# Sums of four rows of V, q and k as TensorE products with bands of ones

## The chip, the cores and the metric

The kernel runs on one core of a Trainium2 chip. The metric is the device time of one execution in microseconds (us), the median of repeated runs; lower is better.

## The reference

Three blocks follow each other. The first, attention, runs for 4 batches of 8 heads over 576 positions of 64 features; the second and third are dense products whose weights are far larger.

```python
q_d = q.reshape(B, H, Sd, 4, D).mean(axis=3)     # Sd = 144; the same for k and v
out_d = sm_attn(q_d, k_d, v_d)                   # softmax(q_d k_d' / 8) v_d
out_up = np.repeat(out_d, 4, axis=2)
mask = np.abs(pos[:, None] - pos[None, :]) < 4   # a local attention beside it
out_local = softmax(where(mask, q k' / 8, -1e9)) v
x = out_up + out_local                           # heads side by side: 4 x 576 x 512
h = np.maximum(x @ w_in, 0)                      # 512 -> 1024
h = h * sigmoid(conv3(h)) @ w_out                # 1024 -> 512
u = x + (x' @ U @ V)'                            # x is now that h; rank 32 over the positions
out = u + np.maximum(u @ w_ch1, 0) @ w_ch2       # 512 -> 2048 -> 512
```

The change is in the first lines: the sums of four neighbouring rows of q, k and V that stand behind the means.

## The kernel before

The heads are worked on two at a time: 16 pairs, p = 0 to 15, four pairs to a batch. One pair has its two heads (h = 0, 1) in the two halves of the 128 partitions.

Of q and k, a load brings 96 rows to each of six column blocks (`load_qk`, tiles qr and kr, two buffers each). `transposes` turns the six blocks on PE into PSUM (tile tr), `emit_qc` and `emit_kc` copy them to SBUF for the local attention, and `emit_qsum` and `emit_ksum` add groups of four columns with a DVE reduction (tiles qs and ks). qs is then scaled into a block-diagonal tile qdbd by POOL, ACT or DVE. `emit_S` makes the local scores of a pair (tile S, 20 products in ten windows of 64 keys, after a product of the mask with identR), `emit_Sd` the scores of the pooled attention (tile Sd). Maxima on DVE, exponentials on ACT (`emit_E`, `emit_Ed`), normalisation on DVE or POOL (`emit_norm`), then transposes of the probabilities on PE (`emit_T`, tiles P and Pd into T).

V is loaded twice. `load_vw` brings ten windows of 64 rows for each head into vw, a tile with one buffer, in four transfers; the local product O = P V of `emit_PV` reads it (20 products a pair). `load_vr` brings the same rows again into vr, 72 partitions with 2 x 4 rows each; `emit_vd` adds them by fours on POOL, in three instructions, into vd, which `emit_PVd` reads (four products into the same bank). `emit_x` adds the two attentions on DVE, and `prep_x` splits the result into a high and a low part (tile xhl) for the product with w_in.

From there on PE does large products: `g1` with w_in (tile g or gb, 12 products to a part, 48 parts; its first may start when pairs 0 to 3 are through), `g2` with w_out (tile acc), then the third block (L935 to L1027). Weights come as 64-bit words and are decoded on ACT and DVE (`decode`, tiles w1t, wraw, wst) and split (`split_hi` on ACT, `split_lo` on DVE or POOL). All loads are issued on SP's queue, in program order, so a load that waits for its buffer holds those behind it.

The order of everything is a hand-kept list of words, `CFG["SEQ"]`: each word is one step of one pair or part (aqT.3 is the transposes of q of pair 3, alw.3 its load of vw, aPVa.3 and aPVb.3 its V products, aPd.3 its PVd, wd a step of decoding, 1.0 a quarter of the first part of g1), and each engine runs its instructions in that order. Words that begin with d are dummy products of the mask (`spin`) whose result is not used. The banks of PSUM for S, Sd, T and O are taken in turn from one ring of four (`bank`); the transposes of whole q and k have two tiles of their own until g1 begins.

## Time and profile before

| | |
|---|---|
| time, median of 3 runs | 781.85 us (780.24 to 782.37) |
| profiled execution | 780.98 us, its span 779.1 us |
| PE busy | 745.5 us, 96% of the span |
| DVE, ACT, POOL busy | 432.3, 339.7, 176.9 us |
| DMA | 51.03 MB, 66 GB/s in the mean |

Busy time is the time in which an engine has at least one instruction in work. A PE that is busy is not a PE at its peak: its matmuls are pipelined, so the distance between two starts is the better price of one. A product of 32-bit numbers is two PE instructions in the trace, so the 20 products of a pair are counted as x40; a transpose is one. The columns of the views by stretches are the busy time of each engine with its number of instructions, then the granted clock of PE, the busy share of the 16 DMA engines and their rate.

### The profile page before, as it was taken

How to read it: one execution, taken by the hardware profiler on the slowest of the kernel's cores; microseconds unless marked ns; L12 is line 12 of the kernel's file. 1: busy time of each engine (PE TensorE's matmuls, PEld its weight loads, DVE VectorE, ACT ScalarE, POOL GpSimd, SP SyncE). 2: the span in 40 equal slices, each digit the busy share in tenths (PEclk: the TensorE clock that was granted, in tenths of full speed). 3: DMA queues.
4: the chain of work that ended last, by engine and by line, in shares of the span. 5: the costliest groups of instructions: out<-in, count | busy, mean ns of one | idle time of the engine just before them, and what ended most of it. 6: DMA issues, size and time to landing. Idle time of an engine off the chain costs nothing.

```text
span 779.1 us, 13059 instructions
## 1 busy us (share of the span) xinstructions
PE 745.5 (96%) x5068; PEld 663.4 (85%) x5068; DVE 432.3 (55%) x827; ACT 339.7 (44%) x1023; POOL 176.9 (23%) x246
## 2 busy tenths in 40 slices
PE   5678999999999999999999999999999999999997
PEld 4556878889888888998898999999899999989996
DVE  6899898888887888899987312211221221122111
ACT  4678978787666766677444212111111211111110
POOL 2357656534336151113611000000000000000000
PEclk9999999999999999999999999999999999999999
DMA  9779664354232122111243100000010000001001
GB/s 227 158 169 205 154 132 96 80 93 92 60 115 53 52 82 82 54 44 39 87 156 121 57 1 1 19 22 1 1 40 1 1 16 25 1 1 41 1 0 42
DMA packets 82450, 51.03 MB, mean 66 GB/s; under 512 B 62013, under 2 KB 74581, under 8 KB 82389
## 3 DMA queue, kind: packets, MB, share of 16 engines
q1 hardware_dynamic: 82388, 50.21, 25.6%
q8 instruction: 40, 0.66, 0.3%
q14 instruction: 22, 0.17, 0.1%
HBM read 45.47 MB, written 4.72 MB: 64 GB/s over the span
## 4 chain that ended last, share of the span: by engine, by line
PE 79%; DVE 11%; ACT 7%; issue 1%; DMA 1%; SPq 0%; POOL 0%; DVEq 0%; ACTq 0%; POOLq 0%
PE acc L1027 25%; PE gb L1008 12%; PE g L1008 12%; PE acc L901 10%; PE g L839 8%; PE gb L839 3%; ACT P L491 2%; DVE hc L875 2%; PE O L594 2%; DVE w1t L217 1%; PE S L477 1%; PE tr L385 1%; PE Sd L513 1%; PE O L605 1%; PE ut L994 1%
## 5 line engine op out<-in xcount | busy, mean ns | idle before, releaser
L1027 PE MATMUL acc<-w,a 128*128 128x512 f32 x864 | 215.0, 393 | 0.0
L1027 PEld LDWEIGHTS acc<-w,a 128*128 128x128 f32 x864 | 161.0, 188 | 29.4 <-DVE a L1017 0.2
L901 PE MATMUL acc<-w,ghl 128*128 128x512 f32 x432 | 111.4, 396 | 0.1
L1008 PE MATMUL g<-uT,w 128*128 128x384 f32 x576 | 111.2, 339 | 0.0
L1008 PE MATMUL gb<-uT,w 128*128 128x384 f32 x576 | 110.9, 339 | 0.0
L1008 PEld LDWEIGHTS g<-uT,w 128*128 128x128 f32 x576 | 101.9, 188 | 4.0
L1008 PEld LDWEIGHTS gb<-uT,w 128*128 128x128 f32 x576 | 101.7, 188 | 3.2 <-POOL w L229 0.2
L1017 DVE SCALAR_TENSOR_TENSOR a<-gb,a 128x384 fp32r<-128x384 f32 x48 | 26.7, 557 | 131.5 <-ACT a L1016 131.5
L839 PE MATMUL g<-xhl,w 128*128 128x386 f32 (+1 forms) x456 | 93.6, 345 | 0.6 <-ACT hc L850 0.3
L901 PEld LDWEIGHTS acc<-w,ghl 128*128 128x128 f32 x432 | 79.5, 188 | 14.7 <-POOL ghl L892 0.5
L1017 DVE SCALAR_TENSOR_TENSOR a<-g,a 128x384 fp32r<-128x384 f32 x48 | 26.7, 557 | 116.5 <-ACT a L1016 116.5
L839 PEld LDWEIGHTS g<-xhl,w 128*128 128x128 f32 x456 | 79.6, 189 | 5.2 <-ACT hc L850 1.8
L1016 ACT ACTIVATE a<-gb 128x384 fp32r<-128x384 f32 x48 | 23.5, 490 | 136.0 <-PE gb L1008 119.6
L1016 ACT ACTIVATE a<-g 128x384 fp32r<-128x384 f32 x48 | 23.5, 490 | 133.3 <-PE g L1008 133.3
L875 DVE SCALAR_TENSOR_TENSOR hc<-hc,cw 128x384 f32<-128x384 f32 x96 | 65.4, 684 | 8.4 <-ACT hc L869 6.4
L491 ACT ACTIVATE P<-S,nm 122x64 f32<-122x64 f32 x160 | 47.7, 317 | 5.6 <-DVE nm L484 5.2
L892 POOL TENSOR_TENSOR ghl<-hc,ghl 128x384 fp32r<-128x384 f32 x21 | 25.3, 1207 | 92.8 <-ACT ghl L889 53.6
L879 ACT ACTIVATE hc<-hc 128x384 f32<-128x384 f32 x48 | 25.0, 524 | 21.4 <-DVE hc L875 20.9
L491 ACT ACTIVATION_READ_ACCUMULATOR P<-S,nm 122x1 f32 x160 | 33.6, 210 | 0.0
L889 ACT ACTIVATE ghl<-hc 128x384 fp32r<-128x384 f32 x48 | 25.2, 524 | 18.5 <-DVE hc L884 17.0
L884 DVE SCALAR_TENSOR_TENSOR hc<-hc 128x384 f32<-128x384 f32 x48 | 30.3, 635 | 4.8 <-ACT hc L879 4.4
L869 ACT ACTIVATE hc<-hc,cw 128x384 f32<-128x384 f32 x48 | 29.5, 615 | 0.9
(135 smaller groups left out, 1013.3 us busy)
## 6 DMA issues: line engine op xcount, KB each, us to landing
wraw<-in_moe_w_ch_dram SPq DMA_DIRECT2D x29, 512.0 KB
qr<-in_q_dram SPq DMA_DIRECT2D x32, 144.0 KB
kr<-in_k_dram SPq DMA_DIRECT2D x32, 144.0 KB
vr<-in_v_dram SPq DMA_DIRECT2D x16, 288.0 KB
out_dram<-u SPq DMA_DIRECT2D x17, 256.0 KB
w1t<-in_moe_w_in_dram SPq DMA_DIRECT2D x8, 512.0 KB
w1t<-in_moe_w_out_dram SPq DMA_DIRECT2D x8, 512.0 KB
vw<-in_v_dram SPq DMA_DIRECT2D x32, 128.0 KB
```

Of the source, the lines that this page charges most:

```text
L491: nc.scalar.activation(out=e["P"][:, i, h], in_=e["S", h][:122, i], func=AF.Exp, bias=e["nm"][:, h, i:i + 1], accum_out=e["sm"][:, i, h:h ...
L839: nc.tensor.matmul(p[:, :wd], w[:, a, cc], xhl[g, cc][:, b, :wd], start=k == 0, stop=k == 3 * NCC - 1)
L869: nc.scalar.activation(out=flat(g, c), in_=inner(g, hts[n], 0), func=AF.Copy, scale=cw[:, f:f + 1])
L875: nc.vector.scalar_tensor_tensor(out=o, in0=inner(g, hts[n], k), scalar=cw[:, k * NF + f:k * NF + f + 1], in1=o, op0=ALU.mult, op1=ALU.add)
L884: nc.vector.scalar_tensor_tensor(out=o, in0=o, scalar=1.0, in1=inner(g, hts.pop(n), 1), op0=ALU.add, op1=ALU.mult)
L889: nc.scalar.activation(out=t[:, 0], in_=cts[n], func=AF.Copy)
L892: eng.tensor_tensor(ghl[n][:, 1], cts.pop(n), ghl[n][:, 0].bitcast(F32), op=ALU.subtract)
L901: nc.tensor.matmul(acc[g][c], t[:, a, c * P:(c + 1) * P], w[:, b], start=f == 0 and i == 0, stop=f == NF - 1 and i == 2)
L1008: nc.tensor.matmul(p[:, :TB], w[:, a, cc], uT[g, cc][:, b, :TB], start=k == 0, stop=k == 3 * NCC - 1)
L1016: nc.scalar.activation(out=t[:, 0], in_=p[:, :TB], func=AF.Relu)
L1017: nc.vector.scalar_tensor_tensor(out=t[:, 1], in0=p[:, :TB], scalar=0.0, in1=t[:, 0].bitcast(F32), op0=ALU.max, op1=ALU.subtract)
L1027: nc.tensor.matmul(acc2[g][c], t[:, a, c * P:(c + 1) * P], w[:, b], start=f == 0 and i == 0, stop=f == NF2 - 1 and i == 2)
```

## The change

For pairs 0 to 7 the second load of V and the three additions on POOL are gone. Instead `emit_Vp` multiplies the windows in vw with bands of ones: for each of ten windows and two heads one product, the band (64 rows, 72 columns) as weights and the window's 64 features moving, added up in two PSUM banks, one per head (tile vp). `emit_Vc` copies the two banks to vd, on ACT, DVE or one on each. Four bands are built on POOL at the start (sixteen small memsets and selects, with those of `fours`). vd now lies with contiguous groups, so `emit_T` takes contiguous columns of Pd for these pairs.

For q and k of pairs 0 to 3 `pooled` makes the sums on PE: the six blocks as weights, as for their transposes, and a 96 x 24 matrix of ones in fours as the moving side. The scaling into qdbd then reads PSUM, on DVE or ACT, and ks is copied from PSUM on DVE or ACT. The word aksa now means this copy on ACT (it was the same as aks before).

The list of words is new as a whole. It has 2585 words instead of 2579; besides the new words, some evictions, normalisations, subtractions and weight splits change their engine, and there are five dummy products instead of seven.

```diff
-        "akT.0 aqv.0 akc.0 aS.0 aks.0 dq.1 aM0.0 wl.1 wd.1 wo.2 aM1.0 aE14.0 aE02.0 aSd.0 wd.1 aE04.0 aMd.0 wd.1 "
...
+    SEQ="wl.0 wd.0 dS.0 wd.0 wd.0 wd.0 lc C wl.2 wd.2 wd.2 wd.2 wh.0 wd.2 wh.2 wo.2 alq.0 aqT.0 aqp.0 aqc.0 aqs.0 "
+        "aVp.1 aVcv.1 aPVa.1 aE0.3 wd.7 akc.4 wd.7 aPd.1 aPVb.1 aT0.2 axd.1 axa.1 ax.1 wh.7 wo.7 av0.2 aS.4 aT1.2 "
...
@@ -274,6 +275,31 @@
         nc.gpsimd.memset(t[:, S:], 0.0)
         qTs.append(t)
 
+    NVP, NG = 8, 72
+    band = p0.tile([P, 4, 160], F32, name="band")
+    nc.gpsimd.memset(band, 0.0)
+    for i, (a, ng) in enumerate(((0, 14), (1, 15), (3, 14), (8, 14))):
+        t = band[:, i, NG:NG + 32].rearrange("p (h x) -> p h x", h=2)[:, :, :ng]
+        nc.gpsimd.memset(t, 1.0)
+        nc.gpsimd.affine_select(out=t, in_=t, pattern=[[-64, 2], [-4, ng]], base=-a, channel_multiplier=1,
+                                compare_op=ALU.is_ge, fill=0.0)
+        nc.gpsimd.affine_select(out=t, in_=t, pattern=[[64, 2], [4, ng]], base=3 + a, channel_multiplier=-1,
+                                compare_op=ALU.is_ge, fill=0.0)
+    NPQ = 4
+    fours = p0.tile([96, 24], F32, name="fours")
+    nc.gpsimd.memset(fours, 1.0)
+    nc.gpsimd.affine_select(out=fours, in_=fours, pattern=[[-4, 24]], base=0, channel_multiplier=1,
+                            compare_op=ALU.is_ge, fill=0.0)
+    nc.gpsimd.affine_select(out=fours, in_=fours, pattern=[[4, 24]], base=3, channel_multiplier=-1,
+                            compare_op=ALU.is_ge, fill=0.0)
+    GROUP = [0] + [(QB * i - i % 2 * 2) // 4 for i in range(1, 9)] + [130]
+    BAND = [0] + [2 - i % 2 for i in range(1, 9)] + [3]
     PT = pa.tile([P, 5, 122], F32, name="PT")
 
     X = {}
@@ -385,6 +411,14 @@
                 nc.tensor.transpose(view[c // 3][:, (c % 3) * 96:(c % 3 + 1) * 96],
                                     e[nm + "r"][:, c].rearrange("p h d -> p (h d)"), ident[:96, :96])
 
+    def pooled(p, nm):
+        e = st[p]
+        t = e[nm + "4"] = whole_tile(p, nm)[:, 0, 288:288 + SD]
+        for c in range(6):
+            nc.tensor.matmul(t[:, 24 * c:24 * c + 24], e[nm + "r"][:, c].rearrange("p h d -> p (h d)"), fours,
+                             start=True, stop=True)
     def like(ap, src):
 
         return ap if len(src.shape) == 2 else ap.rearrange("p (a x) -> p a x", a=2)
@@ -409,14 +443,18 @@
         if not 0 <= p < NPAIR:
             return
         e = st[p]
-        if "qs" not in e:
-            e["qs"] = p0.tile([P, SD], F32, name="qs", tag="qs")
-        qs = e["qs"]
-        for c, src in e["qps"]:
-            nc.vector.tensor_reduce(out=like(qs[:, c.start // 4:c.stop // 4], src), in_=quads(src),
-                                    op=ALU.add, axis=AX.X)
-        if c.stop < S:
-            return
+        if "q4" in e:
+            qs = e["q4"]
+            eng = "DVE" if eng == "Pool" else eng
+        else:
+            if "qs" not in e:
+                e["qs"] = p0.tile([P, SD], F32, name="qs", tag="qs")
+            qs = e["qs"]
+            for c, src in e["qps"]:
+                nc.vector.tensor_reduce(out=like(qs[:, c.start // 4:c.stop // 4], src), in_=quads(src),
+                                        op=ALU.add, axis=AX.X)
+            if c.stop < S:
+                return
         qd = qdbds[p % 2]
         for h in range(2):
             dst = qd[64 * h:64 * h + 64, :, 48 * h:48 * h + 48]
@@ -436,13 +474,16 @@
         for c, src in e["kps"]:
             copy(like(e["kT"][:, c], src), src)
 
-    def emit_ksum(p):
+    def emit_ksum(p, copy=nc.vector.tensor_copy):
         if not 0 <= p < NPAIR:
             return
         e = st[p]
         if "ks" not in e:
             e["ks"] = p0.tile([P, SD], F32, name="ks", tag="ks", bufs=2)
         ks = e["ks"]
+        if "k4" in e:
+            copy(ks, e["k4"])
+            return
         for c, src in e["kps"]:
             nc.vector.tensor_reduce(out=like(ks[:, c.start // 4:c.stop // 4], src), in_=quads(src),
                                     op=ALU.add, axis=AX.X)
@@ -457,6 +498,23 @@
             nc.gpsimd.tensor_tensor(vr[:, h, :, 0:2], vr[:, h, :, 0:2], vr[:, h, :, 2:4], op=ALU.add)
         nc.gpsimd.tensor_tensor(vd, vr[:, :, :, 0], vr[:, :, :, 1], op=ALU.add)
         e["vd"] = vd
+    def emit_Vp(p):
+        e = st[p]
+        e["vps"] = [bank([P, 512], "vp") for _ in range(2)]
+        for i in range(10):
+            c = i // 5
+            for h in range(2):
+                x = NG * (c + 1) + 16 * h - GROUP[i]
+                nc.tensor.matmul(e["vps"][h][:NG, c * D:c * D + D], band[64 * h:64 * h + 64, BAND[i], x:x + NG],
+                                 e["vw"][64 * h:64 * h + 64, i], start=i % 5 == 0, stop=i % 5 == 4)
+    def emit_Vc(p, copies):
+        e = st[p]
+        vd = e["vd"] = pa.tile([72, 2, 2, D], F32, name="vd", tag="vd", bufs=2)
+        for h, copy in enumerate(copies):
+            copy(vd[:, h].rearrange("p c d -> p (c d)"), e["vps"][h][:NG, :2 * D])
 
     def emit_S(p):
 
@@ -560,7 +618,8 @@
                                     e["P"][:, SB[m].start + j].rearrange("p h x -> p (h x)"), ident[:122, :122])
         for j, x in enumerate(((), (0, 1), (2, 3, 4, 5))[m]):
             c = 96 * j + (248 if m == 1 else 0)
-            nc.tensor.transpose(ps[:72, c:c + 96], e["Pd"][:, x // 2, x % 2::2], ident[:96, :96])
+            cols = slice(NG * (x % 2), NG * (x % 2) + NG) if p < NVP else slice(x % 2, None, 2)
+            nc.tensor.transpose(ps[:72, c:c + 96], e["Pd"][:, x // 2, cols], ident[:96, :96])
 
     def emit_Tc(p, m, copy=nc.scalar.copy, copy2=None):
         if not 0 <= p < NPAIR:
@@ -702,7 +761,8 @@
         "kT": (3, lambda p: transposes(p, "k")), "qT": (4, lambda p: transposes(p, "q")),
         "kT0": (3, lambda p: transposes(p, "k", 0)), "kT1": (3, lambda p: transposes(p, "k", 1)),
         "qT0": (4, lambda p: transposes(p, "q", 0)), "qT1": (4, lambda p: transposes(p, "q", 1)),
-        "kc": (3, lambda p: emit_kc(p, A)), "kv": (3, lambda p: emit_kc(p, V)), "ks": (3, emit_ksum), "ksa": (3, emit_ksum),
+        "kc": (3, lambda p: emit_kc(p, A)), "kv": (3, lambda p: emit_kc(p, V)), "ks": (3, emit_ksum), "ksa": (3, lambda p: emit_ksum(p, A)),
+        "kp": (3, lambda p: pooled(p, "k")), "qp": (4, lambda p: pooled(p, "q")),
         "qc": (4, emit_qc), "qv": (4, lambda p: emit_qc(p, True)), "qs": (4, emit_qsum), "qsv": (4, lambda p: emit_qsum(p, "DVE")), "qsa": (4, lambda p: emit_qsum(p, "ACT")),
         "lq": (5, lambda p: load_qk(p, "q")), "lk": (4, lambda p: load_qk(p, "k")),
         "lw": (1, load_vw), "lv": (2, load_vr), "vd": (1, emit_vd),
@@ -723,6 +783,8 @@
             for j in range(5):
                 OPS[f"E{m}{j}"] = 2, lambda p, m=m, j=j: emit_E(p, m, j)
     OPS["S"] = 2, emit_S
+    OPS["Vp"], OPS["Vc"] = (0, emit_Vp), (0, lambda p: emit_Vc(p, (A, A)))
+    OPS["Vcv"], OPS["Vcb"] = (0, lambda p: emit_Vc(p, (V, V))), (0, lambda p: emit_Vc(p, (A, V)))
 
 
     NK = conv_w.shape[0]
```

Two places of PE's order. First the start, from the transposes of pair 0 on (tr: transposes of qr and kr; S and Sd: scores). Before:

```order
L368 MATMUL tr<-mask,identR 128x320
L385 MATMUL tr<-ident,qr 128x96 x6
L385 MATMUL tr<-ident,kr 128x96 x6
L471 MATMUL S<-mask,identR 128x320 x2
L477 MATMUL S<-kT_128,qT_131 58x64 x20
L368 MATMUL tr<-mask,identR 128x320
L513 MATMUL Sd<-ks,qdbd_129 96x144 x3
L385 MATMUL tr<-ident,kr 128x96 x6
L385 MATMUL tr<-ident,qr 128x96 x6
```

The same place now (fours: the sums of q and k):

```order
L411 MATMUL tr<-ident,qr 128x96 x6
L419 MATMUL tr<-fours,qr 128x24 x6
L411 MATMUL tr<-ident,kr 128x96 x6
L419 MATMUL tr<-fours,kr 128x24 x6
L394 MATMUL S<-mask,identR 128x320
L529 MATMUL S<-mask,identR 128x320 x2
L535 MATMUL S<-kT_128,qT_131 58x64 x20
L394 MATMUL tr<-mask,identR 128x320
L571 MATMUL Sd<-ks,qdbd_129 96x144 x3
```

The sums of pairs 0 and 1 have come in behind each transpose, and fewer dummy products stand between. The second place is between the V products of pair 1 and of pair 2 (O<-PT,vw: V product, the only reader of vw before). Before, the first row being pair 1's and the last pair 2's:

```order
L594 MATMUL O<-PT,vw 64x58 x20
L471 MATMUL S<-mask,identR 128x320 x2
L477 MATMUL S<-kT_128,qT_131 58x64 x20
L559 MATMUL T<-ident,P 128x122 x3
L385 MATMUL tr<-ident,kr 128x96 x6
L559 MATMUL T<-ident,P 128x122 x2
L563 MATMUL T<-ident,Pd 72x96 x2
L385 MATMUL tr<-ident,kr 128x96 x3
L513 MATMUL Sd<-ks,qdbd_129 96x144 x3
L385 MATMUL tr<-ident,qr 128x96 x6
L563 MATMUL T<-ident,Pd 72x96 x4
L594 MATMUL O<-PT,vw 64x58 x4
```

Now, from pair 1's PVd to pair 2's V product (vp: the sums of V of pair 2, which read vw as well):

```order
L664 MATMUL O<-PTd,vd 64x144 x4
L653 MATMUL O<-PT,vw 64x58 x4
L617 MATMUL T<-ident,P 128x122 x3
L529 MATMUL S<-mask,identR 128x320 x2
L535 MATMUL S<-kT_128,qT_131 58x64 x20
L617 MATMUL T<-ident,P 128x122 x2
L622 MATMUL T<-ident,Pd 72x96 x6
L411 MATMUL tr<-ident,qr 128x96 x6
L411 MATMUL tr<-ident,kr 128x96 x6
L571 MATMUL Sd<-ks,qdbd_129 96x144 x3
L510 MATMUL vp<-vw,band 72x64 x20
L653 MATMUL O<-PT,vw 64x58 x20
```

The sums of V stand right ahead of the V product of their pair, and the reload of the one vw buffer, which waits for the V product of the pair before, has to land ahead of them.

## Rows read from the trace of the kernel before

**Rows 1.** The page: PE's busy time; the chain that ended last, by engine.

```profile
PE 745.5 (96%) x5068; PEld 663.4 (85%) x5068; DVE 432.3 (55%) x827; ACT 339.7 (44%) x1023; POOL 176.9 (23%) x246
...
PE 79%; DVE 11%; ACT 7%; issue 1%; DMA 1%; SPq 0%; POOL 0%; DVEq 0%; ACTq 0%; POOLq 0%
```

**Rows 2.** Busy time of each engine by stretches (us from the start).

```profile
core 0: us, PE busy (x) PEld busy (x) DVE busy (x) ACT busy (x) POOL busy (x), PEclk, DMA share, GB/s
...
9.43:40.00 30.57, 22.17 (x232) 19.72 (x234) 24.96 (x49) 17.67 (x75) 8.76 (x11) 1.00 0.85 184
...
46.83:70.61 23.78, 17.12 (x298) 13.66 (x296) 22.57 (x47) 19.83 (x87) 15.11 (x20) 1.00 0.74 172
70.61:155.29 84.68, 81.96 (x933) 70.36 (x931) 73.92 (x171) 69.13 (x279) 54.09 (x77) 1.00 0.59 126
155.29:779.10 623.81, 618.47 (x3576) 555.15 (x3576) 299.28 (x537) 225.51 (x566) 92.04 (x112) 1.00 0.15 44
```

**Rows 3.** PE in order of time: start, us, what, idle before it.

```profile
10.06 1.16 PE L385 MATMUL tr<-ident,qr 96*128 96x96 f32 x6
11.01 1.17 PE L385 MATMUL tr<-ident,kr 96*128 96x96 f32 x6
...
27.82 0.84 PE L559 MATMUL T<-ident,P 122*128 122x122 f32 x3 [4.74 <-DVE P L547]
...
40.24 0.72 PE L605 MATMUL O<-PTd,vd 72*64 72x144 f32 x8
...
61.01 0.66 PE L385 MATMUL tr<-ident,qr 96*128 96x96 f32 x6
...
70.61 0.60 PE L839 MATMUL g<-xhl,w 128*128 128x386 f32 x2
```

**Rows 4.** Two short stretches, columns as in rows 2.

```profile
10.00:15.00 5.00, 4.59 (x57) 4.07 (x57) 4.05 (x8) 1.72 (x3) 1.88 (x3) 1.00 1.37 203
...
44.00:45.00 1.00, 0.97 (x7) 0.58 (x5) 1.00 (x4) 0.57 (x2) 0.00 (x0) 0.50 1.08 180
```

**Rows 5.** PE in order of time at the faster clock.

```profile
80.75 0.79 PE L477 MATMUL S<-kT,qT 64*58 64x64 f32 x40
81.47 0.47 PE L385 MATMUL tr<-ident,qr 96*128 96x96 f32 x3
...
84.34 0.98 PE L513 MATMUL Sd<-ks,qdbd 128*96 128x144 f32 x6
85.15 0.42 PE L385 MATMUL tr<-ident,qr 96*128 96x96 f32 x3
...
89.21 0.72 PE L605 MATMUL O<-PTd,vd 72*64 72x144 f32 x8
89.86 1.14 PE L594 MATMUL O<-PT,vw 64*64 64x58 f32 x32
90.93 0.43 PE L559 MATMUL T<-ident,P 122*128 122x122 f32 x2
...
97.13 0.44 PE L594 MATMUL O<-PT,vw 64*64 64x58 f32 x6 [0.23 <-DMA vw<-in_v_dram]
```

**Rows 6.** SP's queue in order of time: the four loads of pair 5.

```profile
91.04 2.58 SPq L306 DMA_DIRECT2D vw<-in_v_dram  x4
```

**Rows 7.** The chain that ended last, 38 to 48 us: start, us, what.

```profile
44.92 2.84 DMA vw<-in_v_dram
```

**Rows 8.** DVE by line and form: count, busy us, mean ns, idle before.

```profile
L447 DVE TENSOR_REDUCE ks<-tr 128x144 f32<-128x576 f32 x6 | 4.5, 746 | 0.0
...
L229 DVE TENSOR_TENSOR w<-w1t,w 128x512 fp32r<-128x512 f32 x5 | 3.3, 684 | 0.7 <-ACT w L225 0.7
```

**Rows 9.** POOL by line and form.

```profile
L457 POOL TENSOR_TENSOR vr<-vr 72x256 f32<-72x256 f32 x32 | 28.2, 900 | 6.4 <-DMA vr<-in_v_dram 6.1
```

**Rows 10.** Waits of SP's queue: us in total, times, longest.

```profile
SPq L316 <- POOL vd L458: 33.3, 7, 9.8
```

**Rows 11.** The page: one kind of load, its count and size.

```profile
vr<-in_v_dram SPq DMA_DIRECT2D x16, 288.0 KB
```

More of the change, by code (lines that the diff above doesn't have):

```diff
@@ L21 @@
     NSA=5, NSB=12,
-    SEQ="dk.0 wl.0 wd.0 wd.0 wd.0 wd.0 wh.0 wO.0 alq.0 lc C wl.2 wd.2 wd.2 wd.2 wd.2 wh.2 dq.0 aqT.0 aqs.0 alk.0 "
[140 rows of a table removed]
+    SEQ="wl.0 wd.0 dS.0 wd.0 wd.0 wd.0 lc C wl.2 wd.2 wd.2 wd.2 wh.0 wd.2 wh.2 wo.2 alq.0 aqT.0 aqp.0 aqc.0 aqs.0 "
[141 rows of a table added]
 @with_exitstack
```

279 rows, old and new, of the table SEQ are left out of this document.

## The prediction

> **What bounds the kernel now.** I read three views in turn. First the page: PE is busy for 745.5 of 779.1 us, and 79% of the chain that ended last is PE's [rows 1]. So a gain can only come out of what PE does not use, and whatever the change adds to PE has to be paid for there. Second, the busy time by stretches [rows 2]: from the first product with w_in at 70.61 us on, PE is busy for 81.96 of 84.68 us and then for 618.47 of 623.81, so it hardly waits again. Before that it waits a lot: 30.57 us hold 22.17 of PE, and 23.78 us (46.83 to 70.61) hold 17.12, while DVE has 22.57 there. So the end is set by two things: when PE reaches its first w_in product (call it g1), and how much PE work is left then. Third, PE's own order of time [rows 3]: pair 0's last product with V ends at 40.24 + 0.65 = 40.9 us, and until about then PE is slow. Six transposes take 1.16 us at 10.06 and 0.66 at 61.01. The column of the granted clock prints 1.00 up to 40 us, but the durations are those of the stretch where it prints 0.50 [rows 4]: PE ran at the 1.2 GHz level, and at 2.4 GHz from 40 us on but for one such stretch.
>
> **PE work.** Prices at 2.4 GHz, from start to next start [rows 5]: 32 instructions of the V product in 90.93 - 89.86 = 1.07 us, so the 40 of one pair 1.34; the four PVd products 89.86 - 89.21 = 0.65; Sd 85.15 - 84.34 = 0.81; the 40 instructions of S 0.72. A Vp (20 sums, two instructions each, weights of 64 rows, 64 columns moving) is nearest to the V product: 64 rows and 64 columns too, and the two heads in the two halves of the rows, two at a time. I take 1.34 us a pair; alone, one at a time, it would be twice that, 2.7. A `fours` product has the same stationary matrix as a transpose of q or k and 24 columns in place of 96; six of them (12 instructions) cost between 0.2 us (at S's 18 ns each) and 1.0 (at the transposes' 0.08 each, half of (11.01 - 10.06) / 6 in [rows 3]). I take 0.5, as the weights to be loaded are the transposes'. All eight sets stand ahead of g1: 4 us. Two of the dummy mask products fewer give back 0.4.
> After g1 the sum is short. Four Vp stand there: 4 x 1.34 = +5.4. But the new order has also put ahead of g1 what stood behind it: pair 3's V products and PVd (1.34 + 0.65), one more Sd (0.81) and seven transposes of the probabilities (some 0.7): -3.5. Left behind g1: **+1.9 us**. g1 must therefore start 1.9 us before 70.6 for the change to cost nothing.
>
> **When g1 starts: DVE.** DVE was the fullest engine ahead of it. Eight reductions of q and k (0.75 each, 6.0) go; four weight subtractions of 0.68 go to POOL or later (2.7) [rows 8]; three normalisations go to POOL and some decoding goes later, against eight scalings, two copies and three evictions of V's sums that come: some 3 us less. In all about 12 us less DVE ahead of pair 3's output, so DVE alone would let g1 start near 58.6. POOL loses 24 additions of 0.9, some 21.6 us, for pairs 0 to 7 [rows 9] and gains five normalisations and the building of the bands, about 4 us ahead of the first use, beside loads that PE waits for anyway: nothing on the path. ACT gets five evictions and five exponentials more and loses as much in copies and decoding; I count it at nothing, hidden while it is 83% busy (19.83 of 23.78) [rows 2]; without that cover it would be some 2 us. Eight loads of 288 KB go [rows 11], and with them half of the 33.3 us in which SP's queue stood at a load of vr waiting for POOL's vd [rows 10], with everything behind it.
>
> **When g1 starts: the reload of vw.** What is late next? The buffer of V's windows exists once. Before, only the V product read it; the sums had vr. Now pair p's sums, their eviction and PVd stand behind the load too, and the load cannot be issued until pair p-1's last V product has ended. So a chain runs over three pairs: load, Vp, V product and PVd. The load: four issues take 2.58 us [rows 6] and the data landed 2.84 us after an issue [rows 7], 5.4 in all. From above, in a crowded stretch, 90.93 (end of pair 4) to 97.13 (PE let go by the load of pair 5) [rows 5]: 6.2. I take 5.4, since 0.9 MB less is moved in this stretch, and keep 6.2. Per pair 5.4 + 1.34 + 1.34 + 0.65 = 8.7, three times 26.2, and then one Sd and the transposes (1.5) ahead of g1: 27.7 us from the end of pair 0's V products to g1. In the order the PE work between (4.1 us for pair 2) does not fill a reload, so PE does wait there.
> Pair 0: PE now has about 18 us of work (by the prices above) up to the end of that product, against 13. It starts at 9.4 us. At 1.2 GHz throughout it ends at 9.4 + 36 = 45.4. If the clock rises at 20 us, because PE has the extra work and fewer gaps (before, a normalisation on DVE alone held it for 4.74 us [rows 3]; it is on POOL now), 5.3 us are done by then and 12.7 follow: 32.7, and with some 4.8 us of waits **37.5**. I take that, keeping 35 and 45.4. g1 then starts at 37.5 + 27.7 = 65.2, 5.4 us earlier than now, later than DVE's 58.6, so the reload decides. Sum against the profiled execution (780.98 us: span 779.1 and 1.9 around it): 780.98 - 5.4 + 1.9 = **777.5 us**. This execution lies 0.87 below the median of the three runs, 781.85, inside their spread.
>
> **Rivals.** (a) A larger gain: pair 0 is through at 35 and a reload takes 4.6 (most of the issues fall beside the landing): 35 + 3 x 7.9 + 1.5 = 60.2, T = 780.98 - 10.4 + 1.9 = 772.5. For it speaks DVE's 12 us; against it that reloads of 4.6 are not in the trace.
> (b) Nothing gained: reloads of 6.2 (+2.4), or as much in new waits for the PSUM banks, of which each of eight pairs now takes two more from the same ring: 780 to 783.
> (c) The slow clock stays. The trace speaks for this: between 10 and 15 us PE was busy for 4.59 of 5 us and yet stayed at the 1.2 GHz level [rows 4]. If it stays there to the end of pair 0's products, they end at 45.4 and T = 777.5 + 7.9 = 785.4, slower. It decides from a rise later than about 27 us: by then 8.8 of the 18 us are done, pair 0's products end at 41 with the waits and g1 starts at 68.7, where the gain is gone.
> (d) The sums with bands run one at a time, because their output spans 72 columns of the array where the V product's spans 64: 2.7 a pair, +5.4 after g1 and +4.0 in the chain: 786.9. S speaks against it: there too two heads write the same output rows in two banks, and 40 instructions take 0.72 us [rows 5].
> A page speaks for a milder form of (d). The Trainium skill, TensorE: Matmul & The Clock Gate, section "Wait — 56ns, not 53.3ns?", says that with decoding in software the sequencer spends about 62 ns on each matmul, which becomes the bound when the array's work is shorter; by that a Vp of 40 would take 2.5 us, and the sum would be 785.6 us. The trace does not agree: S's 40 instructions take 18 ns each.
>
> **Chances.** Forecast 0.40, (a) 0.13, (b) 0.24, (c) 0.15, (d) 0.08, of which 0.02 for the page's rule. About 0.3% (2.3 us) is what a measurement of this kernel tells from no change, so faster means under 779.5 and slower over 784.2. The forecast's own spread puts 0.05 of it into "same", the early end of (b) lies at the edge, and (b)'s late end reaches over it: faster 0.48, same 0.27, slower 0.25. The range leaves out half of (a)'s far end and half of (d): 771 to 787.
>
> **What the profile of the changed kernel would show.** g1 near 65 us and the stretch from there to the end some 2 us longer than 708.5; a Vp of 1.3 us (2.7 by (d)); PE waiting for vw ahead of the Vp of pairs 1 to 3, one or two us each; six transposes at 0.66 from about 20 us on (1.16 until 40 by (c)); DVE no longer at 95% ahead of g1. I am wrong if g1 starts after 68.7, or if PE waits behind g1 for more than the few us it does now.

## The result, and the profile after

The changed kernel takes 793.98 us (793.12 to 795.32) against 781.97: the ratio is 1.0145, 95% interval 1.0120 to 1.0171. It is 12 us slower, and the time lies 7 us above the top of the predicted range.

From the page of the changed kernel, PE's busy time and the chain that ended last by engine (before: [rows 1]):

```profile
PE 772.8 (98%) x5482; PEld 693.4 (88%) x5482; DVE 425.0 (54%) x823; ACT 338.4 (43%) x1022; POOL 171.5 (22%) x255
...
PE 91%; DVE 4%; DMA 2%; ACT 2%; SPq 1%; issue 1%; POOL 0%; DVEq 0%; ACTq 0%; POOLq 0%
```

DVE's share of the chain has fallen from 11% to 4% and ACT's from 7% to 2%. PE has taken their place. The stretches, with the columns of [rows 2] (from the first transpose to the end of pair 0's V products, from there to g1, and the rest):

```profile
core 0: us, PE busy (x) PEld busy (x) DVE busy (x) ACT busy (x) POOL busy (x), PEclk, DMA share, GB/s
9.89:53.30 43.41, 41.79 (x389) 39.20 (x389) 22.68 (x50) 20.89 (x90) 11.95 (x11) 0.72 0.59 134
53.30:86.33 33.03, 29.93 (x488) 25.51 (x487) 25.50 (x58) 24.74 (x114) 14.20 (x23) 0.86 0.64 140
86.33:791.30 704.97, 700.13 (x4608) 628.16 (x4606) 371.45 (x703) 289.44 (x815) 137.41 (x184) 1.00 0.19 52
```

The first product with w_in, g1, starts at 86.33 us; it was 70.61, and 65.2 was forecast. What follows g1 is shorter than before, 704.97 against 708.49. So the loss stands ahead of g1 as a whole, 15.7 us, and 3.5 come back behind it. PE in order of time there (start, us, what; before: [rows 3]):

```profile
10.88 2.65 PE L419 MATMUL tr<-fours,qr 96*128 96x24 f32 x12
...
21.91 1.44 PE L419 MATMUL tr<-fours,qr 96*128 96x24 f32 x12
23.19 0.69 PE L411 MATMUL tr<-ident,kr 96*128 96x96 f32 x6
...
40.60 2.65 PE L419 MATMUL tr<-fours,qr 96*128 96x24 f32 x12
...
46.65 2.67 PE L510 MATMUL vp<-vw,band 64*72 64x64 f32 x40
...
51.44 1.97 PE L653 MATMUL O<-PT,vw 64*64 64x58 f32 x32
...
62.93 1.51 PE L510 MATMUL vp<-vw,band 64*72 64x64 f32 x40
...
86.33 2.55 PE L901 MATMUL g<-xhl,w 128*128 128x386 f32 x12
```

Pair 0's V products end at 51.44 + 1.89 = 53.33 us, where 37.5 was forecast. And the clock, in four of the stretches:

```profile
21.00:24.00 3.00, 3.00 (x28) 2.99 (x28) 1.12 (x2) 3.00 (x16) 1.27 (x1) 1.00 0.03 5
27.00:32.00 5.00, 5.00 (x60) 4.54 (x59) 2.85 (x10) 2.94 (x17) 1.71 (x2) 0.50 1.27 232
36.00:62.00 26.00, 24.48 (x239) 22.07 (x240) 15.01 (x32) 13.16 (x54) 8.20 (x8) 0.50 0.50 120
64.00:86.00 22.00, 19.81 (x383) 16.71 (x380) 18.50 (x43) 17.31 (x81) 11.05 (x19) 1.00 0.63 142
```

The granted clock prints 0.50, the 1.2 GHz level, from 25 to 32 and from 35.5 to 63 us. PE was not resting there: in the third row it is busy for 24.48 of 26 us. (The column prints 1.00 up to the first rise as well; by the durations PE was at the slow level until between 21.0 and 21.9 us.)

### The profile page after: what moved, and what is told of

The parts are those of the page before. It is cut to its first block, busy times and chain, and to the rows that moved or that the text cites. A ratio compares the mean times of both kernels' runs of the same rounds, so it can differ in the third digit from the quotient of the medians.

```text
span 791.3 us, 13883 instructions
## 1 busy us (share of the span) xinstructions
PE 772.8 (98%) x5482; PEld 693.4 (88%) x5482; DVE 425.0 (54%) x823; ACT 338.4 (43%) x1022; POOL 171.5 (22%) x255
## 4 chain that ended last, share of the span: by engine, by line
PE 91%; DVE 4%; DMA 2%; ACT 2%; SPq 1%; issue 1%; POOL 0%; DVEq 0%; ACTq 0%; POOLq 0%
PE acc L1089 25%; PE gb L1070 13%; PE g L1070 13%; PE acc L963 10%; PE g L901 9%; PE O L653 3%; PE tr L411 2%; PE Sd L571 2%; PE gb L901 2%; PE tr L419 2%; PE vp L510 1%; PE S L535 1%; PE O L664 1%; PE T L617 1%; PE h L997 1%; DMA vw<-in_v_dram 1%
## 5 line engine op out<-in xcount | busy, mean ns | idle before, releaser
L1089 PEld LDWEIGHTS acc<-w,a 128*128 128x128 f32 x864 | 161.1, 188 | 29.8
L901 PE MATMUL g<-xhl,w 128*128 128x386 f32 (+1 forms) x456 | 91.7, 343 | 0.7 <-ACT hc L912 0.7
L725 POOL TENSOR_TENSOR xhl<-x,xhl 128x1 fp32r<-128x1 f32 (+2 forms) x52 | 28.1, 566 | 24.7 <-ACT xhl L724 24.6
```

The lines of the kernel that those rows point to most:

```text
L725: eng.tensor_tensor(dst[:, 1, c:c + n], src, dst[:, 0, c:c + n].bitcast(F32), op=ALU.subtract)
L901: nc.tensor.matmul(p[:, :wd], w[:, a, cc], xhl[g, cc][:, b, :wd], start=k == 0, stop=k == 3 * NCC - 1)
L1089: nc.tensor.matmul(acc2[g][c], t[:, a, c * P:(c + 1) * P], w[:, b], start=f == 0 and i == 0, stop=f == NF2 - 1 and i == 2)
```

## What the experiments are, and what they gave

Each kernel was timed against the kernel before on the same chip; the ratios are those to its runs. Each chip has its own runs of the kernel before, with medians from 781.63 to 783.47 us, so the ratios compare kernels better than the times do. g1 and the rest (from g1 to the end) are those of the profiled run, which can lie anywhere among a kernel's runs: e8's (775.33) is its fastest of ten, e13's (785.21) its slowest.

| kernel | us | ratio, 95% interval | g1 | rest |
|---|---|---|---|---|
| before | 781.97 | | 70.61 | 708.49 |
| changed | 793.98 | 1.0145 (1.0120 to 1.0171) | 86.33 | 704.97 |
| e1 no fours | 779.84 | 0.9970 (0.9952 to 0.9988) | 73.15 | 704.75 |
| e2 wide fours | 781.85 | 0.9996 (0.9979 to 1.0013) | 74.14 | 705.76 |
| e15 wide fours twice | 791.95 | 1.0124 (1.0089 to 1.0159) | 85.92 | 704.88 |
| e3 changed, two vw | 790.40 | 1.0097 (1.0058 to 1.0136) | 86.18 | 705.62 |
| e5 = e1, two vw | 778.37 | 0.9948 (0.9927 to 0.9970) | 71.73 | 704.47 |
| e4 before with fours | 794.26 | 1.0149 (1.0111 to 1.0188) | 80.94 | 708.46 |
| e7 before with wide fours | 791.78 | 1.0125 (1.0098 to 1.0153) | 80.94 | 707.26 |
| e8 = e1, 16 dummies | 777.79 | 0.9944 (0.9926 to 0.9961) | 68.61 | 704.99 |
| e10 = e8, two vw | 776.87 | 0.9934 (0.9908 to 0.9959) | 70.86 | 704.44 |
| e17 = e10, scaling on DVE | 776.97 | 0.9921 (0.9900 to 0.9941) | 68.84 | 704.56 |
| e18 = e17, 6 dummies more | 777.69 | 0.9925 (0.9905 to 0.9945) | 69.83 | 704.47 |
| e13 = e8, V's sums 4 to 7 twice | 782.80 | 1.0003 (0.9983 to 1.0023) | 72.15 | 711.35 |
| e14 = e8, V's sums 0 to 3 twice | 781.41 | 0.9988 (0.9967 to 1.0009) | 75.93 | 704.67 |
| e6 = e1, V of 4 to 7 on POOL | 793.50 | 1.0147 (1.0115 to 1.0179) | 73.79 | 719.01 |
| e9 = e6, loads earlier | 787.94 | 1.0068 (1.0042 to 1.0095) | 71.25 | 712.25 |
| e11 = e10 and e9 | 785.70 | 1.0041 (1.0012 to 1.0071) | 71.97 | 713.93 |
| e12 = e9, V of 0 to 7 on POOL | 805.01 | 1.0283 (1.0230 to 1.0336) | 88.51 | 715.39 |
| e16 = e10, V of 8 to 11 on PE | 789.35 | 1.0086 (1.0063 to 1.0109) | 72.32 | 716.48 |

One thing is to be seen at once: with the new order and the sums of V as the change has them, the rest is 704.4 to 705.8 us whatever is done ahead of g1. The profiled runs of those kernels differ by g1 and hardly by what follows.

## The price of the fours and the low clock: e1, e2, e15

e1 takes the fours out:

```diff
-wo.2 alq.0 aqT.0 aqp.0 aqc.0 aqs.0 alk.0 akT.0 akp.0 akc.0 aksa.0
+wo.2 alq.0 aqT.0 aqc.0 aqs.0 alk.0 akT.0 akc.0 aksa.0
```

> The changed kernel without the products with fours: the sums of q and k of pairs 0 to 3 are DVE reductions again, all else and the order stay. In the trace of the changed kernel the eight sets of fours take 15.1 us of PE ahead of the first product with w_in (2.47 us each at the 1.2 GHz level, 1.29 at 2.4). Theory F, they are the loss: pair 0's V products end near 38 us in place of 53.3, the three reloads of V's windows follow, g1 starts at 62 to 70 and the time is 770 to 778. Rival C, PE stays at the 1.2 GHz level to 50 us or more for another reason than the fours: g1 at 74 to 80, 781 to 787. Rival V, the sums of V and their reloads are the loss: g1 stays over 82 and the time over 788.

The time fell by 14 us, to 779.84, and g1 by 13.2. That is theory F by what it removes, but g1 at 73.15 is later than F's 62 to 70, and the time above F's 778. The clock of e1 says why:

```profile
21.00:24.00 3.00, 3.00 (x48) 2.54 (x48) 0.96 (x2) 1.04 (x6) 1.97 (x2) 0.50 0.41 111
...
38.00:46.00 8.00, 7.87 (x85) 6.70 (x82) 4.33 (x13) 3.87 (x18) 3.34 (x3) 0.50 0.40 113
50.00:72.00 22.00, 20.04 (x404) 17.03 (x403) 18.84 (x43) 18.08 (x91) 11.57 (x18) 1.00 0.75 152
```

The low level is there without the fours too, if for shorter: 20 to 27 us, 30 to 33 and, in this run, 37 to 47. It isn't theirs alone.

e2 keeps the fours and makes only their moving side longer:

```diff
-            nc.tensor.matmul(t[:, 24 * c:24 * c + 24], e[nm + "r"][:, c].rearrange("p h d -> p (h d)"), fours,
+            nc.tensor.matmul(full[:, 24 * c:24 * c + 96], e[nm + "r"][:, c].rearrange("p h d -> p (h d)"), wide,
```

> The changed kernel with the moving side of the fours 96 columns in place of 24 (72 columns of zeros, written over by the next product). Theory W, a fours product costs what its 128 columns of weights cost to bring in: 107 ns an instruction at the 2.4 GHz level as now, so the wider product is no dearer than 1.29 us a set there. Rival M, it is priced by what moves: up to four times as long. Beside it, for the clock: if the 1.2 GHz level from 24 to 62 us goes with the short moving side, the granted clock rises for good near 20 to 30 us and the time falls to 778 to 785; if the clock has nothing to do with it, it stays low to about 62 us and the time is 793 to 796.

PE in order of time, and the same four stretches as above:

```profile
11.06 2.77 PE L422 MATMUL tr<-fours,qr 96*128 96x96 f32 x12
...
22.01 1.50 PE L422 MATMUL tr<-fours,qr 96*128 96x96 f32 x12
23.35 0.66 PE L413 MATMUL tr<-ident,kr 96*128 96x96 f32 x6
...
29.67 0.66 PE L413 MATMUL tr<-ident,qr 96*128 96x96 f32 x6
30.17 0.66 PE L413 MATMUL tr<-ident,kr 96*128 96x96 f32 x6
...
44.40 1.14 PE L656 MATMUL O<-PT,vw 64*64 64x58 f32 x32
...
74.14 2.56 PE L904 MATMUL g<-xhl,w 128*128 128x386 f32 x12
```

```profile
21.00:24.00 3.00, 3.00 (x28) 2.99 (x28) 1.16 (x3) 3.00 (x18) 1.27 (x1) 1.00 0.09 13
27.00:32.00 5.00, 3.96 (x72) 3.63 (x71) 4.39 (x12) 4.33 (x24) 2.19 (x2) 1.00 1.27 234
36.00:62.00 26.00, 23.68 (x420) 20.82 (x410) 23.20 (x52) 20.70 (x98) 13.44 (x14) 1.00 0.65 157
64.00:86.00 22.00, 20.72 (x302) 18.46 (x301) 18.92 (x44) 18.32 (x75) 6.80 (x14) 1.00 0.67 150
```

With four times the columns a set of 12 takes 23.35 - 22.01 = 1.34 us from start to start at the faster level, against 1.28 in the changed kernel (21.91 to 23.19). So what moves is not the price, and rival M is out. And PE is at 2.4 GHz from 22 us on and doesn't fall back; the kernel is 12 us faster for doing four times the arithmetic in the fours. This is no accident of the profiled run: the mean granted clock is 0.999 or 1.000 in all ten runs of e2, and 0.977 or 0.978 in all four of the changed kernel. In this order the low level goes with the short moving side.

Theory W is only half shown. The weight loads of the fours last 190 ns at the least with 24 columns moving and with 96, but no run changed the number of weight columns, and that number alone does not set the price: six transposes, with the same 128 columns of weights, take 30.17 - 29.67 = 0.50 us at the faster level, 83 ns each, and their weight loads last 141 ns in the median where those of the fours last 192. Why a transpose's load is shorter stays open.

A page states the price: the Trainium skill, TensorE: Matmul & The Clock Gate, section "LDWEIGHTS (loading the stationary operand)", has a weight load last P / 1.2 ns for P columns, whatever the rows: 107 ns for 128. The trace agrees at the faster level, 1.28 / 12 = 107 ns an instruction, while at the slower one it shows 2.47 / 12 = 206, and it does not agree for the transposes, which come every 83 ns with as many columns. An estimate by the Trainium skill's rule for the eight sets, 96 instructions, is 10.3 us. Another section of that page of the Trainium skill, 'Part 1: The HAM clock gate (the "warmup" mystery)', says that a busy PE is let go to the full clock and an idle one falls back. That doesn't agree as it stands: PE was busy for 24.48 of 26 us at the low level here.

e15 makes each wide product twice:

```diff
+            for _ in range(2):
-            nc.tensor.matmul(full[:, 24 * c:24 * c + 96], e[nm + "r"][:, c].rearrange("p h d -> p (h d)"), wide,
+                nc.tensor.matmul(full[:, 24 * c:24 * c + 96], e[nm + "r"][:, c].rearrange("p h d -> p (h d)"), wide,
```

> e2 (the changed kernel with wide fours, granted clock at 2.4 GHz, 781.85) with each product with fours made twice: 96 instructions more, 107 to 112 ns each. All on the path: 10.3 to 10.7 us, 792 to 792.6. If PE waits for DVE and ACT anyway by then, half of it or less: 784 to 787.

```profile
26.62 2.84 PE L423 MATMUL tr<-fours,qr 96*128 96x96 f32 x24
...
85.92 2.55 PE L905 MATMUL g<-xhl,w 128*128 128x386 f32 x12
```

A set of 24 is now busy for 2.84 us in place of 1.50, g1 starts at 85.92, and the time is 10.1 us more (791.95 against 781.85), where 10.3 to 10.7 is the whole time of the added ones at the faster level (two of the eight sets ran at the slower one and grew by about 2.5 us each). PE's idle time from 10.07 us to g1 is 6.3 us, where e2 has 6.1: the added products took no wait away, so little of them, if any, was hidden. In this order PE is the path ahead of g1, even with the clock up.

## The same fours in the order of before: e4, e7

e4 puts the fours behind the whole transposes of pairs 0 to 3 in the kernel before, unused; e7 the same with 96 columns.

```diff
+        if half is None and p < 4:
+            for c in range(6):
+                nc.tensor.matmul(t[:, 0, 288 + 24 * c:312 + 24 * c], e[nm + "r"][:, c].rearrange("p h d -> p (h d)"),
+                                 fours, start=True, stop=True)
```

> The kernel before with the products with fours added behind each whole transpose of q and k of pairs 0 to 3, their result not used; DVE's reductions stay. Theory F: six to eight sets at 2.47 or 1.29 us, 12 to 18 us of PE, against some 8 us in which PE stands still ahead of pair 0's V products; g1 is 4 to 12 us later and the time 786 to 794. Rival, the fours lie in PE's idle time: 781 to 783. If they also hold PE at the 1.2 GHz level beyond 47 us, g1 is later by another 3 to 8 us.

> The kernel before with the unused fours (794.26) with the moving side 96 columns in place of 24. If the 1.2 GHz level goes with the short moving side also in this order, PE is at 2.4 GHz from 20 to 25 us on, the eight sets cost 1.34 us each, and most of it lies where PE waited for DVE: 781 to 786. If the clock of the changed kernel rose only by its own order, 793 to 796 as with 24 columns.

e4 took 794.26, theory F's top end: the fours alone, in an order that knows nothing of them, cost as much as the whole change. e7 took 791.78, and its expectation of 781 to 786 was wrong. PE in order of time of e4:

```profile
22.10 2.65 PE L396 MATMUL tr<-fours,kr 96*128 96x24 f32 x12
...
47.56 1.44 PE L396 MATMUL tr<-fours,qr 96*128 96x24 f32 x12
...
80.94 1.32 PE L850 MATMUL g<-xhl,w 128*128 128x386 f32 x6
```

and of e7:

```profile
28.71 1.50 PE L398 MATMUL tr<-fours,kr 96*128 96x96 f32 x12
34.74 0.85 PE L572 MATMUL T<-ident,P 122*128 122x122 f32 x3 [4.53 <-DVE P L560]
...
36.34 2.77 PE L398 MATMUL tr<-fours,qr 96*128 96x96 f32 x12
...
80.94 1.30 PE L852 MATMUL g<-xhl,w 128*128 128x386 f32 x6
```

In e4 the slow level lasts to about 47 us by the durations (2.65 and 1.44). In e7 the fours are fast at 28.71, then PE waits 4.53 us for a normalisation on DVE, and behind that wait the fours at 36.34 are slow again (2.77). So a long moving side doesn't keep the clock by itself: with it, too, the clock fell behind a wait. Both profiled runs start g1 at 80.94. Pair 0's V products and PVd were through 3.0 us earlier in e7 (48.07 us against 51.12), and that was lost behind them, where e7's clock was low again from 57.8 to 64.6 and from 71.4 to 78.3 us, e4's only from 53.5 to 60.3. Both are the fastest run of their kernel, e4's (791.23) by 2 us, so the equal g1 says little of the two kernels.

## The reload of V's windows: e3, e5

```diff
-        vw = st[p]["vw"] = pa.tile([P, 10, D], F32, name="vw", tag="vw")
+        vw = st[p]["vw"] = pa.tile([P, 10, D], F32, name="vw", tag="vw", bufs=2)
```

> The changed kernel with two buffers for V's windows, so that the load of a pair need not wait for the V product of the pair before. In the changed kernel the issues and landings of these loads stand in the chain of waits with 10.7 us ahead of g1. Theory: the fours and the slow clock set the start of g1 up to pair 1, the reloads only the last two pairs, where PE stood still for 1.0 us and was given filling work: g1 2 to 5 us earlier, 789 to 792. Rival V, the reload chain is the main loss: g1 10 us earlier or more, under 784. No change if what the loads let go is caught by the next wait: 793 to 795.

> The kernel without fours (779.84) with two buffers for V's windows. Theory: once the fours are gone, the reload chain that the prediction wrote down decides: from 54 to 70 us the chain of waits of that kernel alternates between the issues and landings of V's windows and the products on them, 8.3 and 8.9 us from pair to pair. With a second buffer the loads land early, what is next is DVE (1.7 of 2 us busy there): g1 2 to 5 us earlier, 775 to 778. Rival, DVE and ACT are level with the chain: 779 to 780.5, nothing.

In the changed kernel g1 did not move (86.18): 790.40 by the median, and the two intervals overlap, so e3 shows no gain for certain. Its six runs go from 787.47 to 793.76, at mean granted clocks from 0.991 to 0.978, and the profiled one is the slowest. Without the fours the chain of waits from 50 to 72 us, by line, is this:

```profile
by line: DMA vw<-in_v_dram 26.9%; SPq L330 20.3%; PE O L651 14.3%; ACT P L547 13.3%; PE vp L508 12.5%; PE O L662 6.2%; issue 3.0%; PE T L615 2.2%; PE Sd L569 1.3%; ACT Pd L588 0.9%
```

Loads of vw and their issues are 47% of it, as the prediction's chain had it. Yet the second buffer of e5 brings 1.5 us by the median (778.37 against 779.84, with intervals that overlap) and 1.4 at g1. The chain is there, but DVE and ACT stand level with it: in e5 no load of vw is left in the chain of waits from 44 to 72 us, and pieces of DVE and ACT have taken their place.

## Dummy products for the clock: e8, e10, e17, e18

e8 puts two dummy mask products ahead of each whole transpose of pairs 0 to 3:

```diff
-wo.2 alq.0 aqT.0 aqc.0 aqs.0 alk.0 akT.0 akc.0
+wo.2 alq.0 dq.0 dq.0 aqT.0 aqc.0 aqs.0 alk.0 dk.0 dk.0 akT.0 akc.0
```

> The kernel without fours (779.84; granted clock 0.50 at 20 to 27 and 37 to 47 us) with two more dummy mask products of 320 columns ahead of each whole transpose of q and k of pairs 0 to 3, 16 in all, 0.23 us each at 2.4 GHz, 0.44 at 1.2. If long moving sides let the clock rise, it stays at 2.4 GHz from about 20 us on, pair 0's V products end at 38 to 40 us in place of 43.3 and the time is 775 to 778. If not, they only cost their own time, 3.7 to 7 us less the idle time of PE: 780 to 785.

Two stretches and two rows of PE in order of time of e8:

```profile
22.00:26.00 4.00, 3.78 (x20) 3.70 (x21) 3.86 (x10) 3.68 (x19) 1.10 (x2) 0.50 1.10 304
28.00:68.00 40.00, 33.04 (x631) 28.32 (x632) 35.23 (x77) 30.71 (x142) 19.85 (x28) 1.00 0.72 161
```

```profile
19.19 0.98 PE L570 MATMUL Sd<-ks,qdbd 128*96 128x144 f32 x6 [2.52 <-POOL qdbd L464]
...
68.61 2.55 PE L900 MATMUL g<-xhl,w 128*128 128x386 f32 x12
```

777.79: 2 us faster than e1, in the range expected of a clock that rises. In the profiled run it was up at 13.90 us, where a mask product takes 0.42 us in place of 0.61 at 11.86; e1's was up at 16.79, where six transposes take 0.66. It fell at 20, behind the wait of 2.52 us for POOL's scaling of q's sums, and was back at 27 for good, where e1's fell twice more. Not every run of e8 does as well: the two at a mean granted clock of 0.996 took 775.33 and 776.90, the eight at 0.987 to 0.993 took 777.00 to 779.90. The ten of e1 have 0.981 to 0.989.

e10 adds the second vw buffer; e17 also moves the scaling of pairs 0, 1 and 3 from POOL to DVE (aqs to aqsv); e18 also puts six dummies ahead of pair 1's Sd:

```diff
-aSd.1
+dS.1 dS.1 dS.1 dS.1 dS.1 dS.1 aSd.1
```

> e8 (no fours, 16 dummy mask products, 777.79) with two buffers for V's windows. If the gains of e8 and e5 add up (4.1 and 1.5 against 779.84 minus 2.05 and 1.47): 776 to 777. If DVE is next in both: 777.5 to 778.5.

> e10 (no fours, 16 dummy products, two buffers for V's windows, 776.87) with the scaling of q's sums of pairs 0, 1 and 3 on DVE in place of POOL. PE's wait of 2.9 us at 17 to 20 us falls to below 1.5. Theory: the clock falls behind PE's waits, so it now stays at 2.4 GHz to 30 us or longer, and the time is 773 to 776. Rival: DVE, three scalings of 0.3 us more, is next: 776 to 778.

> As e17, with six more dummy mask products of 320 columns right ahead of pair 1's Sd, where PE waits: they fill up to 2 us of the wait. If the clock stays high for them: as e17 or 1 to 2 us less, 772 to 775. If they only stand in the way: e17 plus 0.5 to 1.5.

776.87, 776.97 and 777.69, by the ratios 0.9934, 0.9921 and 0.9925: all three beat both kernels, by 0.7 to 0.8% against before, and they can't be told from one another. e10's 776.87 is what the sum of the two gains would give, but its interval overlaps with e8's, so that they add up is not shown; e17's scaling and e18's six dummies make no difference that these runs can tell. e17 doesn't test its theory either: PE's wait ahead of pair 1's Sd is still 2.32 us, now for DVE, and with it the clock was up until 29.4 us. In e18 1.89 us of the wait are left, and the clock fell at 19.7. That the clock falls behind PE's waits is thus read from traces (waits of 2.48 us in e1, 4.53 in e7, 2.52 in e8); no run took a wait away, and e17 has one without the fall.

## What a sum of V costs: e13, e14, and five exchanges

e13 makes the sums of V of pairs 4 to 7 twice, e14 those of pairs 0 to 3:

```diff
-        for i in range(10):
+        for i in 2 * list(range(10)) if p in (4, 5, 6, 7) else range(10):
```

> e8 (no fours, 16 dummy mask products, 777.79) with the products of V's sums of pairs 4 to 7 made twice, the second time over the first. Nothing else is added: no load, no eviction. The prediction's theory, PE never rests behind g1: four times 1.31 to 1.45 us, 783.0 to 783.6. Rival, which e6 and e9 speak for: PE is not the bound in this stretch, and the work is hidden: 777.5 to 779.5.

> e8 (777.79) with the products of V's sums of pairs 0 to 3 made twice. They stand in the chain from reload to V product that the prediction wrote down: with all of it on the path four times 1.31 to 1.45 us, 783 to 783.6; if DVE sets the start of g1, one or two of them are hidden: 779 to 781.

The changed kernel's own row, and two of e13's (x80 in place of x40):

```profile
97.00 1.51 PE L510 MATMUL vp<-vw,band 64*72 64x64 f32 x40
98.44 0.98 PE L571 MATMUL Sd<-ks,qdbd 128*96 128x144 f32 x6
```

```profile
82.82 2.81 PE L509 MATMUL vp<-vw,band 64*72 64x64 f32 x80
...
130.74 2.81 PE L509 MATMUL vp<-vw,band 64*72 64x64 f32 x80
```

A Vp is 98.44 - 97.00 = 1.44 us, and e13 costs 5.0 by the medians and 711.35 - 704.99 = 6.4 by the rest: four times 1.25 to 1.6, all on the path. PE's busy time behind g1 is 6.0 us more (706.18 against 700.22), and its waits are not shorter for it. e14 costs 3.6 by the medians, so about two thirds of it lies on the path ahead of g1. There is one more thing in e13. Up to g1 it has the same instructions as e8, yet g1 came at 72.15 in place of 68.61, and from 36 to 48 us its clock was

```profile
36.00:48.00 12.00, 11.87 (x130) 10.37 (x132) 7.05 (x18) 6.80 (x26) 5.49 (x6) 0.50 0.56 143
```

where e8 has 1.00. Whether the clock stays up there differs between runs, and g1 came 3.5 us later with the lower one: single profiles of these kernels are not to be compared closer than that.

The other way to the same price was to give V's sums back to POOL, or to bring more of them to PE, pair by pair:

```diff
-alw.4 aVp.4 aVc.4
+alv.4 alw.4 avd.4
```

This is e6, for pairs 4 to 7. e9 has the second load a pair earlier (alv behind the PVd of the pair before, avd ahead of alw). e11 is e9 with what e10 adds, e12 is e9 for pairs 0 to 7, and e16 brings pairs 8 to 11 to PE in e10 (alw.8 aVp.8 aVc.8).

> The kernel without fours (779.84) with V's sums on PE only for pairs 0 to 3; pairs 4 to 7, whose sums stand behind g1, get their second load and POOL's additions again. Theory: PE never rests behind g1, so each sum there costs its full 1.31 to 1.45 us: 5.2 to 5.8 less, 774 to 774.7. Rival: what they cost is given back as waits for POOL's additions or for the loads on SP's queue: 777 to 780.

> As e6 (no fours, V's sums of pairs 4 to 7 by second load and POOL), but the second loads are put a pair ahead, behind the PVd of the pair before, and the additions ahead of the load of the pair's windows. In e6 PE stood still for 7.9 us waiting for POOL's sums, and the granted clock was 0.90 from 74 to 160 us. Theory: those waits came from the place of the loads; without them the four sums of V are off PE at 1.31 to 1.45 us each: 773.5 to 775.5. Rival: with the sums on POOL PE waits somewhere else as long, since vd, loads and POOL's other work are level with PE there: 780 or more.

> All three together: no fours, 16 dummy mask products, two buffers for V's windows, V's sums of pairs 4 to 7 by early second loads and POOL. If each of the theories holds: 776.5 less 5.2 to 5.8, 770 to 772. If POOL's sums are waited for as in e6: 782 or more.

> The changed kernel's order without any sums on PE: no fours, and V's sums of all 16 pairs by second loads (placed a pair ahead) and POOL. Theory: ahead of g1 the sums of V are cheap on PE (1.3 to 1.45 us a pair beside waits for DVE), so this stands where e9 stands, within 3 us: 772 to 778. Rival: second loads, POOL's additions and PE's waits for them are the dearer way ahead of g1 too: 782 or more, and V's sums on PE are a gain that the fours hid.

> e10 (no fours, dummy products, two buffers for V's windows, 776.87) with V's sums of pairs 8 to 11 on PE as well, their second loads and POOL's additions gone. The prediction's theory: four times 1.31 to 1.45 us more, 782 to 782.7. Rival: a second load with its additions costs more than the sum on PE there too: 776 or less.

All five were slower than what they started from, by 14, 8, 9, 25 and 12.5 us, in both directions of the exchange; e6 and e16 lie above every range that was expected of them. What PE waited for, in us, times and the longest: e6 and e12, one row each of the whole span,

```profile
PE O L662 <- POOL vd L497: 7.9, 3, 4.2
```

```profile
PE O L662 <- POOL vd L497: 11.8, 5, 3.7
```

and e9 behind g1, up to 180 us:

```profile
PE O L662 <- POOL vd L497: 2.7, 2, 1.4
PE O L651 <- ACT Pd L588: 2.2, 1, 2.2
PE tr L409 <- DMA qr<-in_q_dram: 1.6, 1, 1.6
PE T L615 <- ACT kT L473: 1.4, 1, 1.4
```

e1 waits for 0.7 us in that stretch. In e6 and e12 about half of the loss is that PVd waits for POOL's vd; with the loads earlier these waits are 2.7 us in e9, and others, for ACT and for loads of q, have come up in their place. PE's stretch from g1 to the end, of e1, e6 and e9, tells the two sides apart:

```profile
73.15:777.90 704.75, 700.10 (x4608) 627.78 (x4606) 368.33 (x703) 289.07 (x815) 137.79 (x184) 1.00 0.19 52
73.79:792.80 719.01, 702.20 (x4448) 628.25 (x4446) 370.15 (x702) 288.33 (x808) 145.25 (x196) 0.99 0.20 52
71.25:783.50 712.25, 696.64 (x4448) 623.61 (x4446) 373.93 (x704) 287.87 (x808) 147.95 (x196) 1.00 0.20 53
```

In e9 PE is busy for 3.5 us less without the four sums, and idle for 15.6 us in place of 4.7. In e6 it is idle for 16.8 us and, with the four sums gone, still busy for 2.1 us more: its granted clock was 0.50 for 17 us of that stretch. In e16 PE is busy behind g1 for 8.1 us more than in e10, of which four sums at 1.44 are 5.8, and idle for 3.9 us more. So the sums do cost PE their time, and what these five show beside it is the waits, and in e6 the slow clock, that come when a step is taken out of an order that was made around it. e13 and e14 change nothing but PE's work, and their price is the one that counts. Which step brings which of the new waits stays open, and whether V's sums on PE would gain in an order made for POOL's was not tried.

## Why the prediction was wrong

**The fours, a term mis-sized.** The prediction took 0.5 us a set, between 0.2 and 1.0, and 4 us for eight. A set takes 1.28 at 2.4 GHz and 2.47 at 1.2; as it ran, 15.1 us for eight, 10.3 at the faster level. The measured value lies above the upper bound at either level. The failing step is the choice of row. The prediction counted twelve instructions and yet took 0.5 us, six at the transposes' 0.08, because "the weights to be loaded are the transposes'"; but a transpose is one instruction and a product of 32-bit numbers is two, each with its own load of weights. Twelve at 0.08 would have been 1.0, its upper bound, and that falls short too, since an instruction of the fours takes 107 ns where a transpose with the same weights takes 83 (e2). Sd in [rows 5], the nearest 32-bit product among those quoted, has 135 ns an instruction and would have given 1.6, close above what came, but with 96 columns of weights and 144 moving: the closeness would have been luck. And little of the fours' time, if any, was hidden (e15).

**The clock, a rival that should have been the forecast.** The forecast let it rise at 20 us and stay up. It rose between 21.0 and 21.9, fell at 25, was up again from 32 to 35.5, and for good only at 63. Rival (c) had this mechanism, and its evidence, a PE busy for 4.59 of 5 us at the low level [rows 4], was the right one. It was priced at 7.9 us because it was let end with pair 0's products. e2, in which the clock stays up, puts its whole price at 12.2 us of g1 (86.33 to 74.14) and 12.1 of the time.

**From pair 0 to g1.** 27.7 us were forecast for the chain of three reloads; 33.0 came in the changed kernel, 28.7 in e2 (44.40 + 1.07 to 74.14), 29.8 in e8. Once the clock is up the size comes out, but by luck. The sum had PE waiting for vw one or two us a pair; in the changed kernel these waits are 1.0 us in all, and in e2 the view of PE's waits has none for vw: PE is busy for 25.9 of the 28.7 us. The loads are on the chain without the fours (e1), but a second buffer takes off only 1.4 us of it (e5).

**The sum of g1.** 65.2 was forecast and 86.3 came, 21.1 later: 12.2 for the clock, 6.3 for the fours at the faster level and 0.5 for their width in e2, 1.0 in the chain from pair 0 to g1, and 1.1 that I have no name for.

**Behind g1.** +1.9 was forecast, and -3.5 came. The sum of V was right, 1.44 a pair against 1.34, and so was that it costs its whole time there (e13). Rival (d) is out: 1.44 us for 40 is 36 ns an instruction. The Trainium skill, TensorE: Matmul & The Clock Gate, section "Wait — 56ns, not 53.3ns?", which the prediction put beside (d), has about 62 ns a matmul with decoding in software; the trace's 36 ns do not agree with it. What was missed is that PE's idle time in this stretch fell from 8.1 us [rows 2] to 4.8 (704.97 - 700.13): the forecast held PE's few waits there for fixed. PE's busy time is 0.3 us less in place of 1.9 more, so that what the order moved ahead was undercounted by some 2 us.

**The parts at nothing.** DVE's work from the first transposes to g1 fell from 54.25 us to 48.17 (22.7 of 43.4 us and 25.5 of 33.0), 6.1 less where some 12 were forecast. ACT and POOL, taken at nothing, stayed near it: ahead of g1 PE waited 2.1 us for ACT, 1.1 for DVE and not at all for POOL. So in the changed kernel the relief of DVE bought nothing: PE, at half its clock and with 15 us more to do, had become the bound ahead of g1 (busy for 71.7 of 76.4 us, before 44.4 of 61.2). The prediction did add up PE's work up to pair 0's products, 18 us, but with the fours at 1.28 that would have been 24, and behind pair 0 it looked for the bound in the reload and not on PE.

## What to carry to other kernels

Price a product on PE from a row of its own kind, of the same number format and with as many columns of weights, before asking how few columns move: a set of sums over a full 128-column block took 1.28 us here with 24 columns moving, 1.34 with 96, and six transposes of the same weights 0.50. When DVE's work is moved to PE to free the start of a kernel, add PE's work up at the slow clock, since PE may be held there by the very work that is moved; a trial with more columns moving, at no cost in time, shows whether it is. Price an operation by doubling it in place, not by exchanging it in an order that was made around it.

## What the runs showed of the hardware that I had not expected

Making a product do more can make a kernel faster: the fours with 96 columns in place of 24, 72 of them zeros, took 1.34 us a set in place of 1.28 and the kernel 781.85 in place of 793.98, with a granted clock of 1.00 from 36 to 62 us in place of 0.50. With the same 128 columns of weights, an instruction of a 32-bit product took 107 ns and a transpose 83. And two kernels with the same instructions up to g1 started it at 68.61 and 72.15 us, one at 1.00 from 36 to 48 us and the other at 0.50.
